# The first load of x in two token halves, with W1's first block beside it on another queue

## The chip, the cores and the metric

The kernel runs on one core of one Trainium2 chip. The time is the device time of one execution in microseconds (us); lower is better. The profile is one execution seen by the hardware profiler.

## The reference

One token sequence x of 2048 x 640 goes through two branches that a gate mixes:

```python
g = sigmoid((x * gate_w).sum(-1, keepdims=True))
a = A(x, ...)     # complex diagonal state-space layer over the 2048 tokens, 640 states, plus x * Dskip
b = gelu(x @ w1 + b1) @ w2 + b2        # w1: 640 x 1728, w2: 1728 x 640
out = g * a + (1 - g) * b
```

All tensors are bf16. Only the first steps of branch b matter here: x is transposed so that its 640 features lie on partitions, and `x @ w1` is formed.

## The kernel before

**Tiling.** The 2048 tokens are worked in four groups q of 512. The 640 features are five blocks k of 128; F = 1728 is cut into blocks jf of 128. One product of `x @ w1` takes one 128x128 block of `W1sb` as weights and 512 tokens of `xT[q]` as the moving side, and adds up in one bank of PSUM over k = 0..4. For q = 0 the first eight jf blocks are worked k by k (`m1_first`): for each k all eight banks, so that work can begin when only the first block of W1 has come. The other groups, and the later jf, are worked bank by bank (`m1`, line L670), and then come the state-space projections (L713), the second layer (L937, L800) and the output projections (L986, L849).

**Planner.** Every step is an `op` with an engine, a planned duration, tokens that it reads and writes, and a priority. `Sched.order` simulates the engines with these durations and always takes the step with the lowest priority among those whose inputs are there by the plan. The result is a fixed order for each engine; on the chip each engine then runs in that order and waits on semaphores. `load` plans a DMA that is issued from the queue named (SP is SyncE's, ACT is ScalarE's), with `dur` for the issue and `lat` until it counts as landed. A DMA is issued by an instruction at line L333; a transposing DMA (`xtrans`) at L340.

**The start.** The steps around the change, in the order of PE (TensorE) before:

- `warm` (L415): seven matmuls on constants into bank 4, six of 512 columns and one of 256.
- `xt0` to `xt3` (L427): eight transposes of 128x128 of x's feature blocks k = 0 and 1. These two blocks come as they are, in one 256 KB load `xna` into `xn`. Each `xt` is two transposes (256 tokens) and is followed by a copy `xc` on DVE (L433) out of PSUM into `xT[0]`.
- `fill` (L440): two matmuls on constants, into a bank that nobody reads.
- `m1_first` (L648): four products of half the tokens, `(0,0)` and `(0,1)` for tokens 0 to 255 and then for 256 to 511, and then full ones.
- `cols` (L454): one transpose of small vectors loaded into `rows` (b1, Lambda, log_dt); DVE copies the result at L459, and DVE and ACT make the tables of the state-space layer from it.

Feature blocks 2, 3 and 4 of x come by transposing DMAs on SP (`xtrans`). W1's columns 0 to 1023 come in one load for each k, where `WSPLIT` names a column block at which that load is cut in two; all are on SP. The ACT queue issues the four small row loads and `b1b`, and then ACT goes on to its first activation table load (L464).

Of the kernel before, what the change touches and what calls it, by code (L numbers as in the profile page):

```python
# [147 lines left out]
class Prog:  # L148
# [8 lines left out]
    def op(self, name, eng, dur, reads, writes, fn, prio=None, lat=0.0, after=()):  # L157
        deps = {}
        for k in reads:
            for w in self.last_w.get(k, ()):  # L160
                deps[w.idx] = w
        for k in writes:
            for w in self.last_w.get(k, ()):
                deps[w.idx] = w
            for r in self.last_r.get(k, ()):
                deps[r.idx] = r
        for a in after:
            deps[a.idx] = a
        deps = list(deps.values())
        E = self.E  # L170

        def run(eg, deps=deps, eng=eng, fn=fn):
            E.wait(eng, *[d.done for d in deps if not (eng == "pe" and d.eng == "pe")])
            return fn()

        it = self.sch.add(name, eng, dur, deps, run, prio=prio, lat=lat)
        for k in writes:
            self.last_w[k] = [it]
            self.last_r[k] = []
        for k in reads:  # L180
            self.last_r.setdefault(k, []).append(it)
        return it


def bass_gated_mix__ssm_conv_s5__dense_activation_gelu__prompt_kernel(
# [18 lines left out]
    _, S, D = A_x.shape  # L204
    P = A_Lambda_re.shape[0]
    F = B_w1.shape[1]
    assert S % 512 == 0 and D % 128 == 0 and P == D
    KD = D // 128
# [6 lines left out]
    FL = F - (NF - 1) * 128  # L215
# [6 lines left out]
    x2 = A_x[0]  # L222
# [3 lines left out]
    with ExitStack() as es:  # L226

        def SB(name, shape, dt):
            return es.enter_context(nc.sbuf_tensor(name, list(shape), dt))

        xT = [SB(f"xT_{i}", [128, KD, 512], BF16) for i in range(NQ)]
        xn = [SB(f"xn_{i}", [128, 4, D], BF16) for i in range(2)]
# [10 lines left out]
        cols = SB("cols", [128, 3 * KP + NF], FP32)  # L243
# [10 lines left out]
        ident = SB("ident", [128, 128], BF16)  # L254
# [34 lines left out]
        late = [w1f[:, i * D:(i + 1) * D] for i in range(2 * NE + 2 + NO)]  # L289
# [4 lines left out]
        PS = [es.enter_context(nc.psum_tensor(f"ps{i}", [128, 512], FP32)) for i in range(8)]  # L294
# [13 lines left out]
        op = pr.op  # L308

        def inc(eng, ins):  # L310
            return E.inc(eng, ins, eng + "_s")

        def dma_inc(eng, ins, sem):
            SEM(sem)
            E.count.setdefault(sem, 0)
            ins.then_inc(sems[sem], 16)
            E.count[sem] += 16
            return (sem, E.count[sem])
# [7 lines left out]
        def d_mm(n):  # L326
            return n / 2400.0 + 0.004


        def load(name, eng, sem, dst, src, writes, prio, dur=0.5, lat=2.5, reads=(), after=()):  # L330
            def fn():
                with nc.allow_non_contiguous_dma(reason="columns of small vectors"):
                    return dma_inc(eng, engines[eng].dma_start(dst, src), sem)  # L333
            return op(name, eng, dur, reads, writes, fn, prio=prio, lat=lat, after=after)
# [14 lines left out]
        NW = 8  # L349
        FW = NW * 128  # L350
        nmain = (NF - 1) * 128

        def xtrans(q, ks, prio, dur):
            load_T(f"xT{q}_{ks[0]}", f"l_xT{q}_{ks[0]}", [(xT[q][:, ks[0]:ks[-1] + 1, :], x2[q * 512:(q + 1) * 512, ks[0] * 128:(ks[-1] + 1) * 128])],
                   [("xT", q, k) for k in ks], prio, dur)

        WSPLIT = {1: 6, 3: 6}

        def w1load(k, eng, prio):
            edges = [0] + ([WSPLIT[k] * 128] if k in WSPLIT else []) + [FW]  # L360
            for i, (f0, f1) in enumerate(zip(edges, edges[1:])):
                load(f"w1_{k}{i}", eng, f"l_w1{k}{i}", W1sb[:, k, f0:f1], B_w1[k * 128:(k + 1) * 128, f0:f1], [("w1", k, i)], prio=prio + 0.1 * i, lat=2.6)

        def w1tok(k, jf):
            return ("w1", k, int(jf >= WSPLIT.get(k, NW)))

        KN = 2

        load("xna", "sp", "l_xna", xn[0][:, :, 0:KN * 128], x2[0:512, 0:KN * 128].rearrange("(c p) d -> p c d", p=128), ["xna"], 0, dur=0.45, lat=2.0)
        w1load(0, "sp", 1)  # L370
        w1load(1, "sp", 1.3)
        xtrans(0, range(KN, KN + 1), 1.6, 0.8)
        w1load(2, "sp", 2)
        xtrans(0, range(3, 4), 3, 0.8)
        w1load(3, "sp", 4)
        xtrans(0, range(4, 5), 4.5, 0.8)
        w1load(4, "sp", 5)
        FM = FW + 3 * 128
        for i, (f0, f1) in enumerate(((FW, FM), (FM, F))):
            load(f"w1_r{i}", "sp", f"l_w1r{i}", W1sb[:, :, f0:f1], B_w1[:, f0:f1].rearrange("(k p) f -> p k f", p=128), [("w1", "r", i)], prio=20 + i, lat=5.0)  # L380
# [1 line left out]
        ROWS = {"lre": (0, A_Lambda_re), "lim": (KP, A_Lambda_im), "ldt": (2 * KP, A_log_dt), "b1a": (3 * KP, B_b1[0:nmain])}  # L382
# [6 lines left out]
        for i, (nm, (r0, src)) in enumerate(ROWS.items()):  # L389
            src = src.rearrange("(k p) -> k p", p=128)  # L390
            load(nm, "act", "l_" + nm, rows[r0:r0 + src.shape[0], :], src, [nm], prio=-100 + i, dur=0.4)
        load("b1b", "act", "l_b1b", rows[RT:RT + 1, :].rearrange("o (a p) -> o a p", a=2),
             B_b1[nmain:F].rearrange("(o p) -> o p", o=1).unsqueeze(1).broadcast_to([1, 2, FL]), ["b1b"], prio=-101, dur=1.2)

        def f_iota():
            inc("pool", nc.gpsimd.iota(io_i[:, :], pattern=[[1, 128]], base=0, channel_multiplier=-1))
# [13 lines left out]
        one = nc.const_aps.tensor(1.0, [128, 1], BF16)  # L410

        def f_warm():
            t = None
            for n in (512,) * 6 + (256,):
                t = nc.tensor.matmul(PS[4][:, 0:n], one.broadcast_to([128, 128]), one.broadcast_to([128, n]), start=True, stop=True)  # L415
            return inc("pe", t)

        op("warm", "pe", 2.7, (), [("bank", 4)], f_warm, prio=-1000)

        for i, (k, c0, c1) in enumerate(((0, 0, 2), (0, 2, 4), (1, 0, 2), (1, 2, 4))):  # L420
            bank = (7, 6, 5, 4)[i]
            pt = PS[bank][:, :].bitcast(BF16)[:, 0:(c1 - c0) * 128]

            def f_xt(k=k, pt=pt, c0=c0, c1=c1):
                t = None
                for c in range(c0, c1):
                    t = nc.tensor.transpose(pt[:, (c - c0) * 128:(c - c0 + 1) * 128], xn[0][:, c, k * 128:(k + 1) * 128], ident[:, :])  # L427
                return inc("pe", t)

            op(f"xt{i}", "pe", 0.11 * (c1 - c0), ["xna", "ident"], [("bank", bank)], f_xt, prio=-990 + i)  # L430

            def f_xc(k=k, pt=pt, c0=c0, c1=c1):
                return inc("dve", nc.vector.tensor_copy(out=xT[0][:, k, c0 * 128:c1 * 128], in_=pt))  # L433

            op(f"xc{i}", "dve", 0.42, [("bank", bank)], [("xT", 0, k, c0)], f_xc, prio=-2000 + i)

        def f_fill():
            t = None
            for _ in range(2):
                t = nc.tensor.matmul(PS[3][:, 0:256], one.broadcast_to([128, 128]), one.broadcast_to([128, 256]), start=True, stop=True)  # L440
            return inc("pe", t)

        op("fill", "pe", 0.22, ["xna", "ident"], [("bank", 3)], f_fill, prio=-900)

        XK0 = [[("xT", 0, k)] for k in range(KD)]
        XK0[0] = [("xT", 0, 0, 0), ("xT", 0, 0, 2)]
# [6 lines left out]
        def f_cols():  # L453
            return inc("pe", nc.tensor.transpose(psC, rows[:, :], ident[:, :]))  # L454

        op("cols", "pe", 0.3, list(ROWS) + ["b1b", "ident"], [("bank", 7)], f_cols, prio=13.5)

        def f_cols1():
            return inc("dve", nc.vector.tensor_copy(out=cols[:, :], in_=psC[:, 0:RT + 1]))  # L459
# [128 lines left out]
        for ci, src in enumerate((A_B_re, A_B_im)):  # L588
            for i, (p0, p1) in enumerate(((0, 512), (512, KP * 128))):
# [1 line left out]
        xtrans(1, range(KD), 32, 3.4)  # L591
        load("gwb", "sp", "l_gwb", gwb[:, :], gate_w.partition_broadcast(128), ["gwb"], prio=32.2)
        load("xnb", "sp", "l_xnb", xn[0][:, :, KN * 128:D], x2[0:512, KN * 128:D].rearrange("(c p) d -> p c d", p=128),
             [("xn", 0, 0), ("xn", 0, 1)], 32.4, dur=1.0, lat=6.0, reads=["xna"])
        big = load("w2a", "sp", "l_w2a", W2sb[:, 0:NF - 1, :], B_w2[0:nmain, :].rearrange("(j p) d -> p j d", p=128), ["w2a"], prio=33, lat=8.0)
        load("w2b", "sp", "l_w2b", W2sb[0:FL, NF - 1, :], B_w2[nmain:F, :], ["w2b"], prio=34, lat=4.0)
        load("w2c", "sp", "l_w2c", W2sb[64:64 + FL, NF - 1, :], B_w2[nmain:F, :], ["w2c"], prio=34.2, lat=4.0)
# [12 lines left out]
        def pe_prio():  # L610
            ctr["pe"] += 1
            return ctr["pe"]
# [24 lines left out]


        def m1_first():
            seq = [(k, jf) for k in range(KD) for jf in range(NW)]  # L640
            seq.remove((0, NW - 1))
            seq.insert(seq.index((1, NW - 1)), (0, NW - 1))
            steps = [(0, 0, 0), (0, 1, 0), (0, 0, 1), (0, 1, 1)] + [(k, jf, None) for k, jf in seq if k or jf > 1]
            for k, jf, h in steps:
                t0, t1 = (0, 512) if h is None else (256 * h, 256 * h + 256)

                def f_mm(jf=jf, k=k, t0=t0, t1=t1):
                    return inc("pe", nc.tensor.matmul(PS[jf][:, t0:t1], W1sb[:, k, jf * 128:(jf + 1) * 128], xT[0][:, k, t0:t1],  # L648
                                                      start=(k == 0 and t0 == 0), stop=(k == KD - 1), skip_group_check=jf < 2))

                op(f"m1_0_{jf}_{k}_{t0}", "pe", d_mm(t1 - t0), (XK0[k] if h is None else XK0[k][h:h + 1]) + [w1tok(k, jf)], [("bank", jf)],
                   f_mm, prio=pe_prio())
            for jf in range(NW):
                ctr["bank"] += 1

                def f_ge(jf=jf):
                    return inc("act", nc.scalar.activation(Gl[0][:, jf, :], PS[jf][:, :], ACT.Gelu_apprx_tanh, bias=b1col[:, jf:jf + 1]))

                op(f"ge_0_{jf}", "act", d_act(512), [("bank", jf), "b1col"], [("gl", 0, jf)], f_ge, prio=10)
# [442 lines left out]
```

## Time and profile before

| What | Value |
|---|---|
| median of three runs | 213.56 us (212.55, 213.56, 213.62) |
| span of the profiled execution | 211.2 us |
| device time of that same execution | not given apart; the three runs are 1.35 to 2.42 us above the span |
| PE busy | 208.4 us (99%) |
| DVE busy | 190.2 us (90%) |
| ACT busy | 102.9 us (49%) |
| first load of x: issued, in us to landing | 0.74, 3.0 |
| first product (L648) starts | 4.51 us |
| last matmul ends | 209.25 us |

The span runs from the first to the last instruction of the program. PE is matmul, PEld the weight load that goes with it and overlaps it; a wait of PE shows in the PEld rows. SPq and ACTq rows are DMA issues on a queue, not transfers. The column "PEclk" gives the granted clock of PE. Matmul ends are modelled, so the spacing of starts says more than the length of one.

### The profile page before, as it was taken

The page shows a single profiled execution, that of the slowest core. Times are in us where ns is not written, and L with a number is a line of the kernel's source. Part 1 is how long each engine was busy: PE and PEld are TensorE (multiplying, and loading weights), DVE is VectorE, ACT ScalarE, POOL GpSimd, SP SyncE. Part 2 cuts the span into 40 slices and gives each one's busy share as a digit, 9 for nine tenths or more (in the row PEclk, how much of TensorE's full clock was granted, in tenths as well). Part 3 has the DMA queues.
Part 4 walks back from the last instruction along what each step waited for, and adds up shares of the span by engine and source line. Part 5 has one row for each costly group of instructions (what it writes and reads, how often), then busy time and mean ns, then how long its engine had stood idle before and what let it go on. Part 6 is the DMA issues. An engine that isn't in the chain of part 4 may idle for free.

```text
span 211.2 us, 2755 instructions
## 1 busy us (share of the span) xinstructions
PE 208.4 (99%) x1104; PEld 104.3 (49%) x1104; DVE 190.2 (90%) x240; ACT 102.9 (49%) x177; POOL 4.2 (2%) x12
## 2 busy tenths in 40 slices
PE   8999999999999999999999999999999999999996
PEld 3444444444554444444464444444456444567775
DVE  2599999999999999999999999899999999499744
ACT  2588556672990453556680073456660037622330
POOL 1000000030000000000100000000010000000000
PEclk9999999999999999999999999999999999999999
DMA  6899999999930010066074000009542000005251
GB/s 168 203 255 139 193 154 204 310 218 180 218 81 4 0 50 0 0 95 146 10 59 115 3 0 0 0 2 104 114 99 108 0 3 0 0 0 107 69 138 64
DMA packets 48808, 19.08 MB, mean 90 GB/s; under 512 B 41500, under 2 KB 47772, under 8 KB 48796
## 3 DMA queue, kind: packets, MB, share of 16 engines
q1 hardware_dynamic: 47136, 17.59, 41.3%
q0 software_dynamic: 1600, 1.32, 4.5%
q8 instruction: 8, 0.13, 0.3%
q10 hardware_dynamic: 60, 0.01, 0.1%
q14 instruction: 4, 0.03, 0.1%
HBM read 8.41 MB, written 2.63 MB: 52 GB/s over the span
## 4 chain that ended last, share of the span: by engine, by line
PE 99%; DVE 0%; issue 0%
PE ps L670 22%; PE ps L713 20%; PE ps L937 20%; PE ps L986 15%; PE ps L800 7%; PE ps L849 5%; PE ps L648 4%; PE ps L415 1%; PE ps L691 1%; PE ps L948 1%; PE ps L814 0%; PE ps L427 0%; DVE W1sb L883 0%; PE ps L440 0%; PE ps L454 0%
## 5 line engine op out<-in xcount | busy, mean ns | idle before, releaser
L670 PE MATMUL ps<-xT,W1sb 128*128 128x512 bf16 x220 | 48.1, 379 | 0.0
L753 DVE TENSOR_TENSOR_SCAN W<-atab,V 128x1280 bf16<-128x1280 f32 x16 | 44.3, 2812 | 0.3
L713 PE MATMUL ps<-xT,BT 128*128 128x512 bf16 x200 | 43.8, 379 | 0.0
L937 PE MATMUL ps<-Gl,W2sb 128*128 128x512 bf16 (+1 forms) x234 | 42.7, 344 | 0.0
L677 ACT ACTIVATE Gl<-ps,cols 128x512 bf16<-128x512 f32 x44 | 29.9, 694 | 15.5 <-PE ps L670 15.5
L670 PEld LDWEIGHTS ps<-xT,W1sb 128*128 128x128 bf16 x220 | 21.5, 98 | 26.0
L986 PE MATMUL ps<-Hb,CT 128*128 128x512 bf16 x150 | 32.9, 379 | 0.0
L937 PEld LDWEIGHTS ps<-Gl,W2sb 128*128 128x128 bf16 x234 | 22.9, 98 | 19.3
L713 PEld LDWEIGHTS ps<-xT,BT 128*128 128x128 bf16 x200 | 19.5, 98 | 23.8 <-ACT Gt L699 0.4
L722 ACT ACTIVATE U<-ps 128x512 bf16<-128x512 f32 x40 | 23.5, 600 | 14.4 <-PE ps L713 14.3
L955 ACT ACTIVATE E1T<-ps,cols 128x512 bf16<-128x512 f32 (+1 forms) x18 | 9.5, 623 | 33.6 <-PE ps L948 33.6
L986 PEld LDWEIGHTS ps<-Hb,CT 128*128 128x128 bf16 x150 | 14.5, 98 | 17.9 <-DVE V L504 0.6
L994 ACT ACTIVATE E2T<-ps 128x512 bf16<-128x512 f32 x15 | 9.1, 604 | 13.6 <-PE ps L986 13.6
L800 PE MATMUL ps<-W2sb,Gl 128*128 128x320 bf16 x104 | 14.8, 299 | 0.0
L623 DVE SCALAR_TENSOR_TENSOR trf<-xn,gwb 128x640 bf16<-128x640 bf16 x16 | 13.2, 823 | 0.4
L504 DVE TENSOR_TENSOR Hb<-Hb,V 128x1280 bf16<-128x1280 bf16 x16 | 12.5, 822 | 0.3
L504 DVE TENSOR_TENSOR V<-V,W 128x1280 bf16<-128x1280 bf16 x16 | 12.5, 821 | 0.3
L504 DVE TENSOR_TENSOR V<-mr,U 128x2560 bf16<-128x2560 bf16 x8 | 11.9, 1492 | 0.3
L800 PEld LDWEIGHTS ps<-W2sb,Gl 128*128 128x128 bf16 x104 | 10.1, 98 | 4.3 <-issue 0.3
L504 DVE TENSOR_TENSOR Hb<-c,W 128x2560 bf16<-128x2560 bf16 x8 | 11.9, 1490 | 0.2
L974 ACT ACTIVATE xT<-xT,cols 128x512 bf16<-128x512 bf16 x15 | 10.1, 740 | 4.0 <-DMA cols<-in_A_Dskip_dram 4.0
L504 DVE TENSOR_TENSOR W<-mi,U 128x2560 bf16<-128x2560 bf16 x8 | 11.9, 1484 | 0.0
(93 smaller groups left out, 152.0 us busy)
## 6 DMA issues: line engine op xcount, KB each, us to landing
W2sb<-in_B_w_dram SPq DMA_DIRECT2D x1, 2080.0 KB, 9.0
out_dram<-xn SPq DMA_DIRECT2D x3, 640.0 KB, 4.8
xn<-in_A_x_dram POOLq DMA_DIRECT2D x2, 640.0 KB, 7.2
W1sb<-in_B_w_dram SPq DMA_DIRECT2D x3, 256.0 KB, 3.1
trf<-grow SPq DMA_DIRECT2D x3, 256.0 KB, 5.1
xn<-in_A_x_dram SPq DMA_DIRECT2D x1, 640.0 KB, 7.2
W1sb<-in_B_w_dram SPq DMA_DIRECT2D x1, 480.0 KB, 4.0
out_dram<-W1sb SPq DMA_DIRECT2D x3, 160.0 KB, 1.8
```

What stands on the lines that cost most here:

```text
L504: return inc("dve", nc.vector.tensor_tensor(out=o, in0=a, in1=b, op=o_))
L623: t = inc("dve", nc.vector.scalar_tensor_tensor(out=scr[:, :], in0=xn[q % 2][:, c, :], scalar=1.0, in1=gwb[:, :], op0=ALU.mult, op1=ALU.mu ...
L670: t = nc.tensor.matmul(PS[bank][:, :], W1sb[:, k, jf * 128:(jf + 1) * 128], xT[q][:, k, :], start=(k == 0), stop=(k == KD - 1))
L677: return inc("act", nc.scalar.activation(Gl[q % 2][:, jf, :], PS[bank][:, :], ACT.Gelu_apprx_tanh, bias=b1col[:, jf:jf + 1]))
L713: t = nc.tensor.matmul(PS[bank][:, :], BT[:, ci, kd, k * 128:(k + 1) * 128], xT[q][:, kd, :], start=(kd == 0), stop=(kd == KD - 1))
L722: return inc("act", nc.scalar.activation(dst, src, ACT.Copy, scale=1.0 if ci == 0 else -1.0))
L753: t = inc("dve", nc.vector.tensor_tensor_scan(out=g[:, ci, :], data0=a, data1=v[:, ci, :], initial=0.0, op0=ALU.mult, op1=ALU.add))
L800: t = nc.tensor.matmul(PS[bank][:, 0:HALF], Gl[q % 2][:, jf, t4 * 128:(t4 + 1) * 128], W2sb[:, jf, cols], start=False, stop=False, skip_gr ...
L849: t = nc.tensor.matmul(PS[bank][:, 0:n], H[b % NHB][:, ci, k, s * 128:(s + 1) * 128], CT[:, ci, k, cols], start=(i == 0), stop=(i == 2 * K ...
L937: t = nc.tensor.matmul(PS[bank][:, 0:t1 - t0], W2sb[:, jf, d * 128:(d + 1) * 128], Gl[q % 2][:, jf, t0:t1], start=(jf == 0), stop=False)
L974: return inc("act", nc.scalar.activation(xT[q][:, d, :], xT[q][:, d, :], ACT.Copy, scale=cols2[:, 1, d:d + 1]))
L986: t = nc.tensor.matmul(PS[bank][:, :].rearrange("p (s t) -> p s t", s=2), CT[:, ci, k, d * 128:(d + 1) * 128], Hb[:, 2 * (q % 2):2 * (q % ...
```

## The change

- `xna` becomes two loads, `xna0` (tokens 0 to 255) and `xna1` (tokens 256 to 511), both on SP, one after the other.
- W1's block k = 0 goes to the ACT queue, ahead of the small loads, in two halves of four column blocks each. W1's blocks 3 and 4 go to the ACT queue too, behind the small loads, unsplit; block 1 stays on SP, unsplit. `b1b` is now the last of the small loads.
- The transposes of tokens 0 to 255 (both k) come first; those of tokens 256 to 511 get priorities 2.3 and 2.4, among the products, which are numbered from 1. Each transpose waits for its own half only.
- `m1_first` has eight half-token products in place of four: four column blocks for tokens 0 to 255, then the same four for 256 to 511. The products of the last column block for k = 0 and 1 move to just before that of k = 2.
- The filler is gone, and the 256-column matmul of the warm-up. `cols` goes from priority 13.5 to 17.5. The planned durations of the transposing loads go from 0.8 to 1.15.

```diff
-        WSPLIT = {1: 6, 3: 6}
+        WSPLIT = {0: 4}
...
-        load("xna", "sp", "l_xna", xn[0][:, :, 0:KN * 128], x2[0:512, 0:KN * 128].rearrange("(c p) d -> p c d", p=128), ["xna"], 0, dur=0.45, lat=2.0)
-        w1load(0, "sp", 1)
-        w1load(1, "sp", 1.3)
-        xtrans(0, range(KN, KN + 1), 1.6, 0.8)
+        for h in range(2):
+            load(f"xna{h}", "sp", f"l_xna{h}", xn[0][:, 2 * h:2 * h + 2, 0:KN * 128],
+                 x2[h * 256:(h + 1) * 256, 0:KN * 128].rearrange("(c p) d -> p c d", p=128), [("xna", h)], 0.1 * h, dur=0.45, lat=2.0 + 0.7 * h)
+        w1load(0, "act", -120)
+        w1load(1, "sp", 1)
+        xtrans(0, range(2, 3), 1.6, 1.15)
         w1load(2, "sp", 2)
-        xtrans(0, range(3, 4), 3, 0.8)
-        w1load(3, "sp", 4)
-        xtrans(0, range(4, 5), 4.5, 0.8)
-        w1load(4, "sp", 5)
+        xtrans(0, range(3, 4), 3, 1.15)
+        xtrans(0, range(4, 5), 4, 1.15)
+        w1load(3, "act", -90)
+        w1load(4, "act", -89)
...
-             B_b1[nmain:F].rearrange("(o p) -> o p", o=1).unsqueeze(1).broadcast_to([1, 2, FL]), ["b1b"], prio=-101, dur=1.2)
+             B_b1[nmain:F].rearrange("(o p) -> o p", o=1).unsqueeze(1).broadcast_to([1, 2, FL]), ["b1b"], prio=-95, dur=1.2)
...
-            for n in (512,) * 6 + (256,):
+            for n in (512,) * 6:
...
-        for i, (k, c0, c1) in enumerate(((0, 0, 2), (0, 2, 4), (1, 0, 2), (1, 2, 4))):
+        for i, (k, c0, c1) in enumerate(((0, 0, 2), (1, 0, 2), (0, 2, 4), (1, 2, 4))):
...
-            op(f"xt{i}", "pe", 0.11 * (c1 - c0), ["xna", "ident"], [("bank", bank)], f_xt, prio=-990 + i)
+            op(f"xt{i}", "pe", 0.11 * (c1 - c0), [("xna", c0 // 2), "ident"], [("bank", bank)], f_xt, prio=-990 + i if i < 2 else 2.1 + 0.1 * i)
...
-        op("fill", "pe", 0.22, ["xna", "ident"], [("bank", 3)], f_fill, prio=-900)
...
-        op("cols", "pe", 0.3, list(ROWS) + ["b1b", "ident"], [("bank", 7)], f_cols, prio=13.5)
+        op("cols", "pe", 0.3, list(ROWS) + ["b1b", "ident"], [("bank", 7)], f_cols, prio=17.5)
...
-            seq = [(k, jf) for k in range(KD) for jf in range(NW)]
-            seq.remove((0, NW - 1))
-            seq.insert(seq.index((1, NW - 1)), (0, NW - 1))
-            steps = [(0, 0, 0), (0, 1, 0), (0, 0, 1), (0, 1, 1)] + [(k, jf, None) for k, jf in seq if k or jf > 1]
+            late = [(0, NW - 1), (1, NW - 1)]
+            seq = [(k, jf) for k in range(KD) for jf in range(NW) if (k, jf) not in late]
+            i = seq.index((2, NW - 1))
+            seq[i:i] = late
+            steps = [(0, jf, h) for h in range(2) for jf in range(4)] + [(k, jf, None) for k, jf in seq if k or jf > 3]
```

More of the change, by code (lines that the diff above doesn't have):

```diff
@@ L435, in bass_gated_mix__ssm_conv_s5__dense_activation_gelu__prompt_kernel @@
             op(f"xc{i}", "dve", 0.42, [("bank", bank)], [("xT", 0, k, c0)], f_xc, prio=-2000 + i)
[L437 to L441, printed above, removed]
-        op("fill", "pe", 0.22, ["xna", "ident"], [("bank", 3)], f_fill, prio=-900)
         XK0 = [[("xT", 0, k)] for k in range(KD)]
@@ L593, in bass_gated_mix__ssm_conv_s5__dense_activation_gelu__prompt_kernel @@
         load("xnb", "sp", "l_xnb", xn[0][:, :, KN * 128:D], x2[0:512, KN * 128:D].rearrange("(c p) d -> p c d", p=128),
-             [("xn", 0, 0), ("xn", 0, 1)], 32.4, dur=1.0, lat=6.0, reads=["xna"])
+             [("xn", 0, 0), ("xn", 0, 1)], 32.4, dur=1.0, lat=6.0, reads=[("xna", 0), ("xna", 1)])
         big = load("w2a", "sp", "l_w2a", W2sb[:, 0:NF - 1, :], B_w2[0:nmain, :].rearrange("(j p) d -> p j d", p=128), ["w2a"], prio=33, lat=8.0)
@@ L648, in f_mm @@
                     return inc("pe", nc.tensor.matmul(PS[jf][:, t0:t1], W1sb[:, k, jf * 128:(jf + 1) * 128], xT[0][:, k, t0:t1],
-                                                      start=(k == 0 and t0 == 0), stop=(k == KD - 1), skip_group_check=jf < 2))
+                                                      start=(k == 0 and t0 == 0), stop=(k == KD - 1), skip_group_check=jf < 4))
                 op(f"m1_0_{jf}_{k}_{t0}", "pe", d_mm(t1 - t0), (XK0[k] if h is None else XK0[k][h:h + 1]) + [w1tok(k, jf)], [("bank", jf)],
```

## The prediction

> **What bounds the kernel now.** I read the page first: busy shares, then the chain that ended last.
>
> ```profile
> PE 208.4 (99%) x1104; PEld 104.3 (49%) x1104; DVE 190.2 (90%) x240; ACT 102.9 (49%) x177; POOL 4.2 (2%) x12
> PE 99%; DVE 0%; issue 0%
> ```
>
> TensorE (PE) sets the time. The chain of waits, asked for piece by piece, shows one unbroken run of matmuls from about 4.5 us to 209.25 us. The edit touches only what comes before that run and the first 42 products in it (line L648). So I read the chain from 0 to 14 us (start, length, what):
>
> ```profile
> 0.78 2.93 PE ps L415 x7
> 3.71 0.04 issue
> 3.75 0.62 PE ps L427 x8
> 4.38 0.22 PE ps L440 x2
> 4.59 2.46 PE ps L648 x13
> 7.05 0.09 PE ps L454
> 7.14 4.53 PE ps L648 x21
> 11.67 0.05 issue
> ```
>
> L415 is the warm-up on constants, L427 the eight transposes of x, L440 the filler, L648 the products that count. They run at 4.53/21 = 0.216 us each. Then the timeline from 0 to 30 us, for what released each:
>
> ```profile
> 0.74 0.46 SPq L333 DMA_DIRECT2D xn<-in_A_x_dram  x1
> ...
> 0.97 1.19 ACTq L333 DMA_DIRECT2D rows<-in_B_b_dram  x1
> ...
> 2.44 0.15 PEld L415 LDWEIGHTS ps<-const-bfloat16-1.0 128*128 128x128 bf16 x1 [0.28 <-issue]
> ...
> 2.87 0.15 PEld L415 LDWEIGHTS ps<-const-bfloat16-1.0 128*128 128x128 bf16 x1 [0.28 <-issue]
> ...
> 3.75 0.45 PEld L427 LDWEIGHTS ps<-ident,xn 128*128 128x128 bf16 x8 [0.73 <-DMA xn<-in_A_x_dram]
> ...
> 4.08 0.88 DVE L433 COPY xT<-ps 128x256 bf16<-128x256 bf16 x4 [2.16 <-PE ps L427]
> ...
> 4.48 1.21 PEld L648 LDWEIGHTS ps<-xT,W1sb 128*128 128x128 bf16 x9 [0.17 <-DVE xT L433]
> ...
> 11.69 1.42 PEld L648 LDWEIGHTS ps<-xT,W1sb 128*128 128x128 bf16 x8 [0.51 <-issue]
> ```
>
> Three things are to be seen. The transposes start when x lands (3.75), not when the warm-up is done. The first product (4.51) waits for DVE's copy of the first transposes, so the filler lies inside a wait and costs nothing. And the weights for the last eight products (k=4) come late: the 21 products begin at 6.98 in the timeline, 21 x 0.216 ends at 11.51, and the next starts at 11.72. That is a 0.21 us stall which the chain hides in a modelled matmul end; the last 256 KB of W1 were issued at 8.23 and took 3.4 us, landing at 11.6. Last, the DMA view, size and us from issue to landing:
>
> ```profile
> W1sb<-in_B_w_dram SPq DMA_DIRECT2D x3, 256.0 KB, 3.1
> xn<-in_A_x_dram SPq DMA_DIRECT2D x1, 256.0 KB, 3.0
> out_dram<-W1sb SPq DMA_DIRECT2D x1, 128.0 KB, 1.7
> ```
>
> **The order PE will get.** Worked by hand with the planner's own durations: half 0 of x counts as there at 2.45, half 1 at 3.6, W1's first column half at 3.1. The plan is warm-up, xt0, xt1 (half 0, both k), three half-token products, xt2, xt3 (half 1), the fourth half product, four half products of tokens 256 to 511, then full ones. `cols` falls after the sixth product of k=1. PE runs in that order whatever really lands when.
>
> **The change, part by part.**
>
> *Start of the transposes.* The six warm-up matmuls start 0.43 us apart (weight loads at 2.44 and 2.87), so PE is free at 0.78 + 6 x 0.43 = 3.36. Half 0 of x is issued at 0.74. Its landing is bounded above by the whole x (3.0 us: 3.74) and below by the 128 KB store (1.7 us: 2.44). The windows put nearly all DMA traffic of x after 2 us, so I take 3.4, some 0.3 before the whole. Start 3.40 instead of 3.75. The way from first transpose to first product (3.75 to 4.51 = 0.76) is unchanged, as its first copy needs two transposes only. First product at 4.16: **-0.35**. With the ends 3.36 and 3.74 the term is -0.39 to -0.01.
>
> Here a rule speaks against the change. The Trainium skill, "DMA: Bandwidth & Descriptors", section "Issuing engines are not separate DMA queues", says that transfers issued by different engines run on the same 16 DMA engines and interleave, so that a second issuer saves only issue time. By it half 0 shares its way with 128 KB of W1, lands no sooner than the whole did, and the sum below would be 0.34 worse, at +0.43.
>
> *Second pair of transposes.* xt2 and xt3 stood ahead of the first product; now they stand between products. Eight take 0.45 (the weight-load row), four 0.22: **+0.22**.
>
> *Wait for their copy.* The first product of the second token half needs DVE's copy of xt2, again 0.76 after xt2 starts. PE has in that time the four transposes (0.22) and one half product (0.11), and nothing else may pass, since it runs in order. Idle 0.43: **+0.43**. If half 1 lands after 4.16 + 0.33 = 4.49, the difference is added. Issued at about 1.26, with 3.0 us as x took or the 4.0 us of the 192 KB W1 row, it lands at 4.26 to 5.26: 0 to +0.77. I take 0, as its bytes stand where the second half of x stands now.
>
> *W1's first block on ACT.* Its first half is issued near 0.74 and needed at 4.05; at 3.0 to 4.0 us it lands at 3.74 to 4.74: 0 to +0.67. I take 0, the nearest row being the 3.1 of the W1 blocks. ACT's four small loads move back by two issues (about 1.1 us at the 0.54 of a W1 issue), `b1b` with its 1.19 comes last of them, and W1's blocks 3 and 4 follow at about 4.3 to 5.4. The activation table load queued behind them (3.58 now) moves to about 5.4 and ends at 6.7. `cols` comes at about 7.6 instead of 6.93, so ACT still waits for `cols`, not the reverse.
>
> *SP.* It loses four W1 issues of blocks 0 and 3 and 4, saves one by not splitting block 1, and gains one for x, some 2.1 us in all. Its transposed loads come earlier, and the last W1 block leaves ACT at 5.4 instead of SP at 8.23, so even with 4.0 us it lands before 10: the stall at k=4 goes, **-0.21**. The last `xT` load, issued near 5.3 rather than 7.07, is not next to bind.
>
> *Free edits.* No filler: it lay in the wait for the copy. Two more split products: 0.216 as before in two parts. `cols` later by 0.7 delays DVE's whole chain, which is nearly gapless; what covers it is this slack between DVE's last H and the matmuls that read it:
>
> ```profile
> 66.23 1.56 DVE L504 TENSOR_TENSOR Hb<-Hb,V 128x1280 bf16<-128x1280 bf16 x2
> ...
> 71.71 10.90 PE ps L986 x50
> ```
>
> H is done at 67.79, PE reads it at 71.71: 3.9 us cover 0.7. Without cover it would cost 0.7.
>
> **Sum:** -0.35 + 0.22 + 0.43 - 0.21 = **+0.09 us**, on a profiled span of 211.2 us. The page gives no device time for that execution; the runs shown (212.55, 213.56, 213.62) lie 1.35 to 2.42 above the span, and nothing in the edit touches what lies around it. Against the median: 213.65, say 213.7. Half a per cent, 1.07 us, is what a measurement of this kernel can tell from no change; the three runs alone differ by that. With the ends above this case reaches from 213.3 to 214.8.
>
> **Rivals.**
>
> *The clock switches late (slower).* The warm-up runs at 0.43 us per 512 columns, the products at 0.216, though the granted-clock column says 1.00 from the start. The switch falls between 2.87 and 3.75, after some 2.5 to 2.9 us of nearly unbroken PE work. Here that work is cut: six warm-ups, then about 0.3 idle before the first product, then 0.43 more. If the switch needs another unbroken stretch of 2.9 us, that stretch runs at half speed and costs 1.45: 213.65 + 1.45 = 215.1. It decides once the idle pieces make the switch miss its first chance. For: the spread of 1.07 between equal runs fits a switch that moves. Against: in the profiled run it came before the filler was reached. The Trainium skill, "TensorE: Matmul & The Clock Gate", Part 1, puts the clock under a free-running activity window of about 3.4 us, and Part 4 says that transposes don't count as busy in the same way; by an estimate from that page a missed window costs half of 3.4, 1.7 us.
>
> *Both transfers late (slower).* Sharing delays W1's half to 4.74 and x's half 1 to 5.26, together up to +1.2: 214.8. Against: the bytes ahead of them are those of before.
>
> *A gain beyond the sum (faster).* x lands by 3.36 and the plan's idle 0.43 is filled: -0.39 + 0.22 - 0.21 = -0.38, 213.2. If moreover the switch falls early in most runs, where two of the three now seem to pay about 1 us, 212.3. This also covers that the plan comes out otherwise than I worked it.
>
> **How the numbers follow.** Near-equal case 0.48, of which 0.05 beyond +0.5%; clock 0.25; late transfers 0.10; gain 0.17. Faster 0.17, same 0.43, slower 0.05 + 0.25 + 0.10 = 0.40. Signs are mixed, so the range takes in the cheap end of the gain and the clock case: 212.5 to 215.3. The likeliest case's own range is 213.3 to 214.8.
>
> **What would show it.** In the timeline: first L427 weight load near 3.4; first L648 near 4.16 and its first three at 128x256, four transposes after them; one idle of about 0.4 before the fifth; k=4 without a stall, near 11.8. Wrong would be: the transposes still at 3.7 (shared transfer), weight loads of L648 at 0.43 instead of 0.216 (clock), a DMA named before the first product, or L986 waiting for DVE near 71 us.

## The result: slower by 0.7%

The changed kernel took 214.89 us (median of 11 runs, 213.21 to 215.35), the kernel before, on the same chips, 213.16 us (11 runs, 212.55 to 213.63). The ratio is 1.0069, with a 95% interval of 1.0048 to 1.0089; here and below it weighs all runs, so it can differ from the quotient of the two medians. The near-equal case (213.7) did not come; the time lies in the stated range, between the near-equal case and the clock case, and its main cause was in neither.

The page of the changed kernel, busy shares and chain:

```profile
PE 208.9 (98%) x1103; PEld 104.5 (49%) x1103; DVE 190.2 (89%) x240; ACT 103.2 (48%) x177; POOL 4.2 (2%) x12
PE 93%; DMA 4%; SPq 1%; issue 0%; DVE 0%
```

A DMA has entered the chain with 4%. The chain of waits from 0 to 16 us names it (start, length, what):

```profile
4.19 8.06 DMA xT<-in_A_x_dram
12.24 0.05 issue
12.29 3.63 PE ps L643 x16
```

One transposing load of x (block 3) was issued at 4.19 and landed 8.06 us later; the last 16 products at L643 (k=3 and k=4) waited for it. The timeline from 0 to 14 us shows the rest (warm-up is L417 here, transposes L429, products L643):

```profile
0.74 0.91 ACTq L333 DMA_DIRECT2D W1sb<-in_B_w_dram  x2
0.74 0.97 SPq L333 DMA_DIRECT2D xn<-in_A_x_dram  x2
...
3.69 0.34 PEld L429 LDWEIGHTS ps<-ident,xn 128*128 128x128 bf16 x4 [1.10 <-DMA xn<-in_A_x_dram]
...
4.18 0.89 ACTq L333 DMA_DIRECT2D W1sb<-in_B_w_dram  x2
...
4.47 0.34 PEld L643 LDWEIGHTS ps<-xT,W1sb 128*128 128x128 bf16 x3 [0.44 <-DVE xT L435]
...
5.85 2.06 PEld L643 LDWEIGHTS ps<-xT,W1sb 128*128 128x128 bf16 x13 [0.39 <-DVE xT L435]
...
9.36 2.32 PE L643 MATMUL ps<-xT,W1sb 128*128 128x512 bf16 x10 [0.68 <-DMA W1sb<-in_B_w_dram]
...
12.29 1.90 PE L643 MATMUL ps<-xT,W1sb 128*128 128x512 bf16 x8 [0.61 <-DMA xT<-in_A_x_dram]
```

Read by matmul starts, the first product came at 4.48 (before: 4.51), so the start gained 0.03. The first four half products, with the second transposes and the wait for their copy among them, took until 5.85 instead of 0.43 us: +0.94. Of that, 0.22 are the transposes, 0.33 the wait, and 0.39 the slow clock: transposes 0.107 and half products 0.213 apart until about 5.3 us, where the profiled execution of before was at 0.056 and 0.109 from 3.75 on. Then come two stalls, 0.84 before k=2 (8.30 to 9.36 between two starts that need 0.22) and 0.78 before k=3; the 0.21 at k=4 is gone. Together -0.03 + 0.94 + 1.62 - 0.21 = 2.32 of the 2.4 us by which the spans differ (213.6, 211.2). The device time of the profiled execution is 214.89, 1.29 above its span; with the same distance the profiled execution of before took about 212.5 (an estimate), one of its quickest, so the medians differ by less, 1.73.

The DMA view of the issues between 3.4 and 8 us (KB each, us to landing) says which loads are late:

```profile
W1sb<-in_B_w_dram ACTq DMA_DIRECT2D x2, 256.0 KB, 6.6
W1sb<-in_B_w_dram SPq DMA_DIRECT2D x1, 256.0 KB, 5.7
xT<-in_A_x_dram SPq DMA_TRANSPOSE x3, 6.9
```

The transposing loads of x before (the same view in narrower windows, one load each):

```profile
xT<-in_A_x_dram SPq DMA_TRANSPOSE x1, 4.0
xT<-in_A_x_dram SPq DMA_TRANSPOSE x1, 3.0
```

W1's block 2 (SP) needs 5.7 us where it needed 3.1, the transposing loads 6.9 (median of three) where they needed 3.0 to 4.0.

### The profile page after: what moved, and what is told of

Same layout as the page of the kernel before. It is cut to its first block, busy times and chain, and to the rows that moved or that the text cites. A ratio compares the mean times of both kernels' runs of the same rounds, so it can differ in the third digit from the quotient of the medians.

```text
span 213.6 us, 2755 instructions
## 1 busy us (share of the span) xinstructions
PE 208.9 (98%) x1103; PEld 104.5 (49%) x1103; DVE 190.2 (89%) x240; ACT 103.2 (48%) x177; POOL 4.2 (2%) x12
## 4 chain that ended last, share of the span: by engine, by line
PE 93%; DMA 4%; SPq 1%; issue 0%; DVE 0%
PE ps L665 22%; PE ps L708 20%; PE ps L932 20%; PE ps L981 15%; PE ps L795 7%; PE ps L844 5%; DMA xT<-in_A_x_dram 4%; PE ps L643 2%; PE ps L686 1%; SPq L333 1%; PE ps L943 1%; SPq L340 1%; PE ps L809 0%; DVE W1sb L878 0%
## 5 line engine op out<-in xcount | busy, mean ns | idle before, releaser
L665 PE MATMUL ps<-xT,W1sb 128*128 128x512 bf16 x220 | 48.1, 379 | 0.0
L665 PEld LDWEIGHTS ps<-xT,W1sb 128*128 128x128 bf16 x220 | 21.5, 98 | 26.0
L981 PE MATMUL ps<-Hb,CT 128*128 128x512 bf16 x150 | 32.9, 379 | 0.0
L981 PEld LDWEIGHTS ps<-Hb,CT 128*128 128x128 bf16 x150 | 14.5, 98 | 17.9 <-issue 0.3
L498 DVE TENSOR_TENSOR V<-s,W 128x2560 bf16<-128x2560 bf16 x8 | 11.9, 1484 | 0.0
```

The lines of the kernel that those rows point to most:

```text
L498: return inc("dve", nc.vector.tensor_tensor(out=o, in0=a, in1=b, op=o_))
L665: t = nc.tensor.matmul(PS[bank][:, :], W1sb[:, k, jf * 128:(jf + 1) * 128], xT[q][:, k, :], start=(k == 0), stop=(k == KD - 1))
L981: t = nc.tensor.matmul(PS[bank][:, :].rearrange("p (s t) -> p s t", s=2), CT[:, ci, k, d * 128:(d + 1) * 128], Hb[:, 2 * (q % 2):2 * (q % ...
```

## The experiments

Two theories stood after the comparison. **Queue**: W1's blocks 3 and 4, 512 KB that are now issued on ACT at 4.2 us, run beside SP's loads, which are needed sooner, and delay them. **Start**: the split x, the slow clock and the idle pieces before 5.85 us make the loss. Each variant was timed beside the kernel before, and its ratio is to those runs. Landings and matmul starts that no line below shows are read from the trace of the one profiled execution of each variant.

### e1: W1's blocks 3 and 4 back on SP

```diff
-        w1load(3, "act", -90)
-        w1load(4, "act", -89)
+        w1load(3, "sp", 3.5)
+        w1load(4, "sp", 5)
```

> The changed kernel with W1's blocks 3 and 4 issued on SP again, between and behind the transposing loads of x (order of before), all else as changed. Theory 'queue': the two stalls of the changed kernel, 0.84 us before k=2 (W1 block 2, 5.7 us to landing) and 0.78 us before k=3 (transposing load of x block 3, 8.1 us), come from the 512 KB on the ACT queue; both go, block 2 lands in 3 to 4 us again, and the median falls by 1.4 to 1.6 us to 213.3 to 213.5. Rival 'start': the loss is in the slow clock and the idle pieces before 5.85 us; the median stays within 0.5 us of 214.9. First product still near 4.48 in both.

Measured: median 212.95 us, ratio 1.0019 (0.9992 to 1.0045): not told from before, and below the 213.3 to 213.5 expected. The DMA view, same window:

```profile
W1sb<-in_B_w_dram SPq DMA_DIRECT2D x3, 256.0 KB, 4.0
xT<-in_A_x_dram SPq DMA_TRANSPOSE x3, 4.2
```

The windows (us; then length and busy time of PE, PEld, DVE, ACT, POOL; granted clock; DMA share; GB/s) show PE without a gap where the changed kernel stalls:

```profile
8.00:9.00 1.00, 1.00 (x7) 0.46 (x6) 0.53 (x4) 0.31 (x2) 0.00 (x0) 1.00 1.60 264
9.00:10.00 1.00, 1.00 (x6) 0.48 (x5) 0.90 (x4) 0.98 (x2) 0.00 (x0) 1.00 0.72 168
...
11.00:12.00 1.00, 1.00 (x6) 0.48 (x5) 0.95 (x3) 0.98 (x2) 0.00 (x0) 1.00 1.03 321
```

PE's order is that of the changed kernel and the first product still comes at 4.52, but the two stalls are gone. So the issue of these two blocks makes most of the loss, and the start of the change costs 0.45% at the most, the upper end of the interval; e5, below, which has fillers besides, gives 0.19% (0.03 to 0.35). Two things were not expected. The twelve runs spread from 212.72 to 215.30, three of them above 214.4. And the profiled execution (213.79 us) has a stall of 0.86 us at another place, before the first L665 product. Its W1 columns took 6.5 us to landing: 14 of the load's 16 parts had landed by 12.29, the last two at 14.38 and 14.61, though every load in flight then was on SP.

### e2 and e7: only that part, on the kernel before

e2 moves the two loads to ACT in the kernel before. The planner had no other step for ACT at its time zero and put the first part of block 3 (192 KB) ahead of the small loads, issued at 0.74:

```diff
-        w1load(3, "sp", 4)
+        w1load(3, "act", -90)
...
-        w1load(4, "sp", 5)
+        w1load(4, "act", -89)
```

> The kernel before, with one part of the change: W1's blocks 3 and 4 on the ACT queue behind the small loads. Theory 'queue': W1 block 2 and the transposing load of x block 3 take over 5 us to landing, PE stalls 1 to 2 us between 7.5 and 12.5 us, slower than before by 1.0 to 1.6 us. Rival 'start': no stall over 0.3 us, and the 0.21 us stall at k=4 goes: 0 to 0.3 us faster.

Measured: 215.16 us, 1.0079 (1.0048 to 1.0110). Not clean: x landed at 4.39, and the clock stayed slow until about 8.9 us. e7 therefore makes both loads wait, in the plan alone, for the memset that the small loads wait for (`after=[rz]`), so that they come behind them.

> The kernel before with W1's blocks 3 and 4 on the ACT queue behind all small loads (in e2 the planner put the first part of block 3 ahead of them, where it delayed x to 4.4 us). PE's order is that of before. Theory 'queue': W1 block 2 and the transposing load of x block 3 take over 5 us to landing, PE stalls 1 to 2 us in all between 7.5 and 12.5 us; median 214.1 to 215.2. Rival 'it needs the changed start': stalls under 0.4 us, median 212.9 to 213.4.

Measured: 214.59 us, 1.0062 (1.0038 to 1.0086). x lands at 3.75 (before: 3.71), PE's order is unchanged, and the waits from 0 to 16 us show the two stalls again (us in total, times, longest):

```profile
PE ps L648 <- DMA W1sb<-in_B_w_dram: 1.3, 1, 1.3
...
PEld ps L648 <- DMA xT<-in_A_x_dram: 0.6, 1, 0.6
```

By matmul starts the stalls are 1.42 us before k=2 and 0.28 before k=3. The profiled execution (215.20, the slowest of the six) also had a late clock: PE's work before is that of the kernel before, yet full speed came at 5.84 us instead of 3.62, and the products stood 0.89 us behind at `cols`. The stalls alone (1.70, less the 0.21 at k=4 that goes) account for the 1.4 us between the medians.

Taken alone, this part gives nearly the whole loss (1.0062 of 1.0069). Undone, most of the loss goes (e1). That settles which part makes it, up to a remainder of some 0.2% (0.45% at the most).

### e3: the same bytes ahead, in one queue

e1, but with blocks 3 and 4 on SP right behind block 2, priorities 2.2 and 2.4, ahead of the transposing loads of x.

> The changed kernel with W1's blocks 3 and 4 on SP, but right behind block 2 and ahead of the transposing loads of x blocks 3 and 4: the bytes that run ahead of those loads are as in the changed kernel, in one queue. Theory 'two queues mixed': within one queue copies and transposing loads don't run at the same time, so block 3 of x lands by 10 to 11 us, before it is needed (11.5), and the time is that of the order of before, 213.3 to 213.6. Rival 'bytes ahead': it lands as late as in the changed kernel, about 12.2, a stall of 0.6 to 0.8 us stays before k=3, 214.0 to 214.3.

Measured: 213.35 us, 1.0032 (1.0008 to 1.0056). x's block 3 landed at 10.61 instead of 12.24 and no stall was left before k=3, though as many bytes stood ahead of it. The stall before k=2 stayed, 0.67 us by matmul starts: block 2 landed at 8.57. The only wait for a DMA that is left between the products:

```profile
PE ps L643 <- DMA W1sb<-in_B_w_dram: 0.5, 1, 0.5
```

So not bytes alone made x late, but in this execution block 2 suffers even on one queue when block 3 follows it closely. The stall before k=2 thus stays with the early issue alone, and the one before k=3 needs the second queue too; what a later issue on ACT would cost, no run here shows.

### h1: no transposing loads beside the ACT queue

The changed kernel, with x's blocks 3 and 4 as plain copies:

```diff
-        xtrans(0, range(3, 4), 3, 1.15)
-        xtrans(0, range(4, 5), 4, 1.15)
+        for k in (3, 4):
+            load(f"xT0_{k}", "sp", f"l_xT0_{k}", xT[0][:, k, :].rearrange("p (c d) -> p c d", c=4),
+                 x2[0:512, k * 128:(k + 1) * 128].rearrange("(c p) d -> p c d", p=128), [("xT", 0, k)], prio=k, dur=1.15, lat=3.0)
```

> The changed kernel, W1's blocks 3 and 4 on ACT as in the change, with one thing replaced: x's blocks 3 and 4 of the first 512 tokens come by plain copies of the same 128 KB in 256-byte pieces on SP, not by transposing loads (these two blocks are left untransposed, so the products use other data; the amount of work is the same). Theory 'a transposing load beside copies of the other queue': W1's block 2 lands by 8.3 and x's blocks by 10 us, the stalls before k=2 and k=3 shrink from 1.6 us in all to under 0.4, median 213.0 to 213.5. Rival 'two queues sharing, whatever the kind': block 2 still takes over 5 us to landing (past 8.7), stalls of 0.8 us or more stay, median over 214.

Measured: 214.30 us, 1.0047 (1.0028 to 1.0065), as the rival had it that two queues share whatever the kind. Two things come apart here. The windows, first the changed kernel:

```profile
8.00:9.00 1.00, 0.68 (x4) 0.20 (x2) 0.23 (x2) 0.21 (x1) 0.00 (x0) 1.00 0.43 77
9.00:10.00 1.00, 0.64 (x3) 0.32 (x4) 0.90 (x5) 0.74 (x2) 0.00 (x0) 1.00 0.99 128
```

then h1:

```profile
8.00:9.00 1.00, 0.39 (x3) 0.06 (x1) 0.47 (x4) 0.25 (x2) 0.00 (x0) 1.00 1.16 297
9.00:10.00 1.00, 0.00 (x0) 0.00 (x0) 0.90 (x4) 0.98 (x2) 0.00 (x0) 1.00 0.98 311
```

and the kernel before:

```profile
8.00:9.00 1.00, 1.00 (x7) 0.47 (x5) 0.90 (x4) 0.98 (x2) 0.00 (x0) 1.00 0.81 210
9.00:10.00 1.00, 1.00 (x6) 0.41 (x5) 0.97 (x3) 0.93 (x3) 0.00 (x0) 1.00 0.70 126
```

Without transposing loads of x in flight, 297 to 311 GB/s are moved instead of 77 to 128. But the kernel before, with all on SP, moves 210 and 126 (e1 264 and 168): a low rate goes with transposing loads in one queue too, and only in the first window is it lower with the second queue (77 here, 154 in e7). Yet block 2 is as late as ever, 10.03 us, and PE stalls 1.94 us in one piece. The landings in the trace say why: a load is done when the last of its 16 parts has landed. In h1 fourteen parts of block 2 have landed by 7.85 us and the last two at 9.74 and 10.03; in the changed kernel eleven by 6.97, the last at 9.22; in the kernel before all sixteen within 0.11 us (7.16 to 7.27), in e1 within 0.16. Why a few of the parts fall behind stays open. A single queue doesn't exclude it: in e3 two parts of block 2 are 1.4 us late, and the two late parts of e1 are 2.1 to 2.3.

### e4 and e5: fillers in PE's idle pieces

Two 256-column matmuls on constants behind the first four transposes, three behind the fourth half product; e4 on the changed kernel, e5 on e1.

> The changed kernel with PE kept busy in its two short waits: two 256-column matmuls on constants behind the first four transposes, three behind the fourth half product, into banks that are overwritten later. Theory 'cut work delays the clock': weight loads go from 0.43 (per 512 columns) to 0.216 spacing before 4.5 instead of near 5.25 us, and the median falls by 0.3 to 0.8 us. Rival 'clock on its own time': the switch falls where it will, the median moves by less than 0.3 us; the stalls before k=2 and k=3 take up part of either.

Measured: 215.11 us, 1.0101 (1.0069 to 1.0132), the slowest of all by the ratio. In the profiled execution (216.67 us; one other run took 216.56, the rest 214.64 to 215.26) block 2 landed at 10.13, and what followed is in the windows (granted clock is the third number from the end):

```profile
8.00:10.00 2.00, 0.25 (x2) 0.00 (x0) 1.50 (x7) 1.38 (x3) 0.00 (x0) 1.00 0.54 96
10.00:11.00 1.00, 0.74 (x2) 0.28 (x3) 0.97 (x2) 0.91 (x4) 0.00 (x0) 0.66 1.11 116
11.00:12.00 1.00, 1.00 (x4) 0.41 (x3) 0.95 (x3) 1.00 (x1) 0.00 (x0) 0.50 1.24 165
12.00:13.00 1.00, 1.00 (x4) 0.35 (x3) 0.97 (x5) 0.26 (x1) 0.00 (x0) 0.50 1.06 300
13.00:14.00 1.00, 1.00 (x4) 0.40 (x3) 0.90 (x10) 0.00 (x0) 0.00 (x0) 0.63 1.11 359
```

After a 2.0 us wait of PE the clock fell to half, from 10.33 to 13.74 us by the trace, and half of these 3.41 us, 1.7, were lost on top of the stall (an estimate). A late load can thus cost twice. Neither theory had that; as a test of the start, e4 says nothing: its clock had risen at 3.50, ahead of the first filler at 3.99. e5 is that test:

> The kernel of e1 (W1's blocks 3 and 4 back on SP) with the fillers of e4: two 256-column matmuls behind the first four transposes, three behind the fourth half product. In e1 most runs took 212.7 to 213.3 us, but 3 of 12 took 214.5 to 215.3. Theory 'cut work makes the clock miss a chance': with the two idle pieces filled no run is over 214, as in none of the 23 runs of before. Rival 'clock or transfers on their own time': again about a quarter of the runs near 215. The median stays at 212.7 to 213.1 in both.

Measured: 213.59 us, 1.0019 (1.0003 to 1.0035); one of 12 runs over 214 (214.82), against 3 of 12 in e1. Most runs took 213.4 to 213.9, where most of e1's took 212.7 to 213.0: the fillers bring no gain, and the expected median (212.7 to 213.1) was missed. Whether they keep slow runs away, one against three of twelve can't tell.

### e6 and g4: the warm-up alone

e6 is the kernel before without its filler and without the 256-column warm-up; g4 keeps the filler and cuts the warm-up to four matmuls.

> The kernel before without its filler (two 256-column matmuls) and without the seventh warm-up matmul of 256 columns: only that part of the change. Theory 'cut work makes the clock miss a chance': the median stays within 0.3 us of before, but some runs take 1.5 to 2 us more, 214.5 to 215.3. Rival: no run above 214, as before.

Measured: 213.34 us, 1.0001 (0.9987 to 1.0015), no run over 213.72. What the change takes off the warm-up, and the filler, are free.

> The kernel before with a warm-up of four 512-column matmuls instead of six and a half (filler kept): PE then idles from about 2.5 to 3.75 us, and nothing else changes. Theory 'cut work makes the clock miss a chance': most runs at 214 to 215.5, the switch in the profile past 6.5 us in most cases. Rival 'clock on its own time': median within 0.3 us of before, no run above 214.

Measured: 214.57 us, 1.0073 (1.0049 to 1.0097), all six runs over 214. Its PEld rows:

```profile
3.78 0.77 PEld L427 LDWEIGHTS ps<-ident,xn 128*128 128x128 bf16 x8 [2.04 <-DMA xn<-in_A_x_dram]
...
8.45 0.15 PEld L648 LDWEIGHTS ps<-xT,W1sb 128*128 128x128 bf16 x1 [0.28 <-issue]
8.88 0.15 PEld L648 LDWEIGHTS ps<-xT,W1sb 128*128 128x128 bf16 x1 [0.28 <-issue]
...
9.53 0.37 PEld L648 LDWEIGHTS ps<-xT,W1sb 128*128 128x128 bf16 x3
```

Products are 0.43 us apart up to 9.3 us. So the clock case is real: work that is cut enough (2.0 us without a weight load) misses the switch, and that alone costs 0.7%. In the changed kernel's profile the switch came near 5.3 us, so there the cut does not go so far.

### e9: does W1's first half delay x?

e1 with W1's block 0 on SP behind both halves of x, `w1load(0, "sp", 0.5)`, its planned landing set to 1.6 so that PE's order stays.

> The kernel of e1 with W1's first block on SP too, in its two halves behind the two halves of x; nothing but small loads on ACT. Theory 'the first W1 half shares x's way': half 0 of x, alone on the engines, lands 0.3 to 0.5 us earlier than the 3.70 of e1, and the first product starts at 4.1 to 4.25 instead of 4.52. Rival 'the transfer time is fixed cost': it lands within 0.15 us of 3.70. The median is 0.1 to 0.4 below e1's 212.95 in the first case, at most 0.2 off in the second.

Measured: 213.88 us, 1.0044 (1.0018 to 1.0069). The timeline from 2.5 to 5 us:

```profile
3.08 0.58 PEld L429 LDWEIGHTS ps<-ident,xn 128*128 128x128 bf16 x4 [0.49 <-DMA xn<-in_A_x_dram]
...
4.43 0.80 PE L643 MATMUL ps<-xT,W1sb 128*128 128x256 bf16 x3 [0.51 <-DMA W1sb<-in_B_w_dram]
```

Half 0 of x lands at 3.04 instead of 3.70, 0.66 us earlier (3.04 in g1, below, too), so W1's half on the other queue had taken x's way. The gain goes at once into the wait for W1's half (4.29). The time did not fall as expected; the median rose. In the profiled execution half products were still 0.21 us apart at 6.2 us, the slow clock; whether that is the cause is not shown.

### g1 and g2: a version meant to beat both

x half 0, W1's first half, x half 1, the rest of block 0, all on SP in this order; blocks 3 and 4 as in e1; xt2 and xt3 behind two half products. g2 adds fillers (one and two matmuls).

> A version meant to beat both: all of W1 and x on SP, in the order x half 0, first half of W1's block 0, x half 1, the rest of block 0; blocks 3 and 4 between and behind the transposing loads. PE's order as changed, but xt2 and xt3 stand behind two half products. In e9, half 0 of x landed at 3.04 and the product then waited for W1's half (4.29). Theory 'order on one queue': x half 0 lands near 3.0, W1's half by 3.8, the first product starts near 4.05 instead of 4.43 to 4.52; the quick runs at 212.3 to 212.6, and as PE's early work is cut as in e1 and e9, a quarter to a third of the runs at 214.5 to 215.5. Rival 'nothing gained': first product at 4.4 or later, quick runs at 212.8 to 213.

Measured: 213.80 us, 1.0034 (1.0019 to 1.0049). The first product came at 4.09, as the theory had it, but nothing came of it: everything behind on SP is issued about 1 us later than in e1 (block 2 at 4.56 instead of 3.53), block 2 landed at 8.33, and PE stalled 0.43 before k=2 and 0.90 before L665. No run was under 213.1 (expected: quick ones at 212.3 to 212.6), and none over 214.3, so the expected slow quarter did not show either.

> g1 with fillers: one 256-column matmul on constants behind the first four transposes, two behind the fourth half product. Theory 'cut work makes the clock miss a chance': at most 1 of 12 runs above 214.3, median 212.4 to 212.9, 0.1 to 0.4% faster than before. Rival 'clock on its own time': as many slow runs as g1.

Measured: 213.19 us, 1.0014 (0.9997 to 1.0030): not faster than before, against the 0.1 to 0.4% expected. As no run of g1 was above 214.3, g2 could not show whether fillers help against such runs. No kernel of this study beat the kernel before.

## Why the prediction was right or wrong

The time lies in the range (212.5 to 215.3), but by luck: the upper end was the price of the clock case, and two stalls of like size, which no case had, took its place. Near-equal, the likeliest case, did not come.

**The order of PE** came out as worked by hand, to the place of `cols`. **The idle piece** was sized 0.43 and measured 0.33; **the second transposes** 0.22, and 0.33 at the slow clock.

**Start of the transposes, -0.35: mis-sized, -0.06.** Half 0 landed at 3.65, not 3.4. The rule of the Trainium skill that was weighed there ("DMA: Bandwidth & Descriptors", "Issuing engines are not separate DMA queues") put it at 3.74 and was nearer; e9 shows the sharing directly (3.04 alone, 3.70 beside W1 in e1).

**"The stall at k=4 goes, -0.21": the step that failed.** The stall itself did go, but the premise was wrong. The prediction took the 4.0 us of a W1 row of before as the worst landing for a block on ACT ("even with 4.0 us it lands before 10"); block 4 took 7.2 us and landed at 11.87, and PE, 1.62 us late by then, did not need it before 14.0. Worse, it priced only what moved to ACT and the moved loads' own dates. It never asked what the 512 KB would do to the loads that stayed on SP, though the same rule, read for the later loads too, was the hint: block 2 and x's block 3 stalled PE by 0.84 and 0.78 us. "Is not next to bind" was said of the last x load; the one before it bound. The rival "both transfers late" had the mechanism, but for the first halves only, which came in time (W1's first half at 3.33, x's second at 4.40).

**The clock rival** was right as a mechanism (g4) and wrong as the main cause: e1 keeps all of PE's cut work, e6 the cut warm-up and filler, and neither is told from before. In the profiled execution the later switch costs 0.39, but one execution doesn't show that the cut work made it late. The moment moves with the same work as well: 3.62 us in the profile of before, 5.84 in e7's; and with fillers it was 3.50 in e4's and 5.39 in e5's. Whether the slow quarter of e1's runs is a missed switch stays open, as none of them was profiled.

**The ends** of the near-equal case don't follow from its terms: the earliest start (-0.39) gives 213.6, not 213.3, and the three upper ends together (+0.34, +0.77, +0.67) give 215.4, not 214.8.

**Free edits**: confirmed. The filler and the warm-up cost nothing to remove (e6), and `cols`, at 8.24 instead of 6.93 us, did not make the L981 matmuls wait longer for DVE (0.6 us of weight loads' idle time in all, 0.9 before).

## What to carry to other kernels

A load that is moved to a second queue is not early for nothing: here it ran at once, against what the first queue had in flight, and a load needed sooner took 5.7 us instead of 3.1. So price every load that is needed before it. Of the orders tried here, the best kept W1's late blocks in one queue with x, in the order of need (the kernel before and e1). Turning transposing loads into plain copies raised the rate, but did not bring block 2 in sooner (h1). Look at what happens to the last part of a load, not at its bytes: in h1 fourteen of sixteen parts were there by 7.85 us, and PE waited for the last, at 10.03.

## What was not expected of the hardware

- Copies on ACT's queue beside transposing loads on SP's moved 77 to 128 GB/s between 8 and 10 us; plain copies on both moved 297 to 311. The kernel before, with both kinds on SP, moved 210 and 126.
- Of one 256 KB load (W1's block 2), parts landed up to 3.1 us apart (6.90 to 10.03 us in h1) when another queue was busy, and 0.11 us apart in the kernel before. A second queue is not needed for it: in e1 the parts of a 480 KB load lay 2.5 us apart (12.12 to 14.61).
- PE's clock fell to half after a wait of 2.0 us and stayed there 3.41 us (e4, one execution). In h1 a wait of 1.8 us was followed by products at the full rate.
